# Attention in front of routed experts: q, k, v sets in up to four places on chip, loaded one transfer at a time, with five row buffers and another order of the first loads

## The chip, the cores and the metric

The kernel runs on one core of one Trainium2 chip. The metric is the device time of one execution in microseconds (us); lower is better. The kernel before took 1081.59 us (median of 3 runs, 1078.17 to 1083.07). TensorE is called PE here, VectorE DVE, ScalarE ACT, GpSimd POOL and SyncE SP; SP does no arithmetic, it issues transfers (DMAs).

## The reference

Three layers follow one another. The inputs are q, k and v of 4 batches, 8 heads, 576 positions and 64 columns.

```python
scores = scale * np.matmul(q, k.transpose(0, 1, 3, 2))
mask_plain = (rel >= 0) & (rel < 32)                                   # heads 0 to 3
mask_dil = (rel >= 0) & (rel < 128) & (rel % 4 == 0)                   # heads 4 to 7
attn = softmax(np.where(masks, scores, -1e9)); x = np.matmul(attn, v)  # then rows of 512 columns, 2304 of them
logits = x @ w_gate + np.log1p(np.exp(x @ w_noise)) * noise            # the best 2 of 8 experts for each row
out[mask] += top2_w[mask, k, None] * (np.maximum(x[mask] @ w1[e], 0.0) @ w2[e])
g = out @ w_gate2; y = (g * sigmoid(g) * (out @ w_val)) @ w_out
```

## The kernel before

**Stages.** The program is written out by hand in one order, and each engine executes its own instructions in that order. First comes attention with the routing of the first three quarters of the rows woven in (in the trace about 0 to 122 us), then the experts (to about 626 us), then the gated layer (to the end).

**Attention.** A *set* is the q, k and v of one batch b and one half t of the heads (t = 0 plain, t = 1 dilated): eight sets, each of 576 KB of q, 608 KB of k and 877.5 KB of v. A *unit* is two blocks of 64 queries: 36 units, nine for a batch. Units 9b to 9b+3 use set (b, 0), unit 9b+4 uses both, units 9b+5 to 9b+8 use set (b, 1). Unit u is therefore followed by the first use of (1, 0) at u = 9, of (1, 1) at 13, (2, 0) at 18, (2, 1) at 22, (3, 0) at 27 and (3, 1) at 31.

**One step.** `att_step(i)` (L691) is software-pipelined. On PE it issues the scores of unit i+1 (`at_S`: a mask matmul L183, then q times k L190), the product with v of unit i-1 (`at_AV`, L227), the turning of the normalised rows of unit i-2 (`at_XT`, L273) and the turning of the probabilities of unit i (`at_T`, L216). On DVE it issues the row maximum of unit i+1 (L198, L202), some small routing instructions (`go`), and then `at_norm` of unit i-1 (L256, L259, L262), whose last instruction writes the row tile `xs`. SP then stores `xs` to DRAM (`zd`, L267). `xs` has three buffers, so the rows of unit u wait until the store of unit u-3 has landed.

**Loads.** `load_qkv` (L87) issues q, k and v of one set on SP, back to back. The tiles of q, k and v have two buffers each in the pool `at`; so a set's transfers wait until the last reader of the set two before has finished, and SP, which issues in order, waits with them. The calls stand at L905 (before unit 5 of the batch) and L907 (before unit 1 of the batch). `load_raw` (L152) loads expert weights, `split` (L158) makes two parts of them on ACT and POOL. `late_consts` (L133) casts constants on DVE.

Of the kernel before, what the change touches and what calls it, by code (L numbers as in the profile page):

```python
# [20 lines left out]
N, DM, E, FF, F2 = 2304, 512, 8, 1024, 1536  # L21
NT = N // 128          # token tiles
NB = S // 64           # query blocks of one sequence
SEG = S // 4           # positions of one residue class
NA = N // 128          # most slot blocks of one expert
CAP = 640              # slots of one expert on the straight path
EARLY = 256            # first slots of experts 0 and 1, filled by batches 0 and 1 only
LOW = 384              # tokens of one block of the last layer
ID0 = 1024
# [11 lines left out]
def attn_moe_glu_kernel(ctx, tc, qT, kT, vB, cst, wgn, noise, wm, wz, out):  # L41
# [16 lines left out]

    # rows of x by token, then rows of y by slot (block, expert, row); a token with a slot past the
    # straight path finds its combined row in the place of its x  # L60
    zd = dr.tile([N + NA * E * 128, DM], F32, name="zd")
# [21 lines left out]

    # ------------------------------------------------------------ loads
    qt, kt, vt = {}, {}, {}

    def load_qkv(b, t, parts=1):  # L87
        q = qt[b, t] = at.tile([128, 2, S], F32, tag="q", bufs=2, name="q")
        k = kt[b, t] = at.tile([128, 2, 32 + S], F32, tag="k", bufs=2, name="k")
        v = vt[b, t] = at.tile([96, 4, NB, D + 1], F32, tag="v", bufs=2, name="v")  # L90
        cut = [0, S] if parts == 1 else [0, 128, S]
        for a, z in zip(cut, cut[1:]):
            SP.dma_start(q[:, :, a:z], qT[b, t, :, :, a:z])
            a2, z2 = (a + 32 if a else 0), z + 32
            SP.dma_start(k[:, :, a2:z2], kT[b, t, :, :, a2:z2])
            if z == cut[1]:
                SP.dma_start(v, vB[b, t])

    # dense work for the array while the first loads are on their way
    fill = gp.tile([128, 512], BF16, tag="g_ob", bufs=1, name="fill")  # L100
# [7 lines left out]
    busy(WARM[0])  # L108
    A.preload_act_table_set("natural_log_exp_and_others")
    ccon = gp.tile([128, C_MASK], F32, name="ccon")  # L110
    zs = gp.tile([128, N], F32, name="zs")
    SP.dma_start(ident, cst[:, 0:128])
    SP.dma_start(zs[:, 0:C_END - C_MASK], cst[:, C_MASK:])
    load_qkv(0, 0, parts=2)
    SP.dma_start(ccon[:, 128:C_MASK], cst[:, 128:C_MASK])
    wg = gp.tile([128, 4, 32], F32, name="wg")
    SP.dma_start(wg, wgn)
    nz = gp.tile([128, NT, E], F32, name="nz")
    SP.dma_start(nz, noise)
    load_qkv(0, 1)  # L120

# [22 lines left out]

    # ------------------------------------------------------------ expert weights
    segs = [(0, 0, EARLY), (1, 0, EARLY), (0, EARLY, CAP), (1, EARLY, CAP)] \
# [18 lines left out]

    # ------------------------------------------------------------ attention
    units = []
# [63 lines left out]
    def pieces(subs):  # L231
        """(partition, type, first token, step, count) of the rows of a unit"""
        res = []
        for sub, (t, j) in enumerate(subs):
            p = j * 64
            while p < j * 64 + 64:
                if t == 0:
                    n = j * 64 + 64 - p
                    tok, st = p, 1
                else:  # L240
                    n = min(j * 64 + 64, (p // SEG + 1) * SEG) - p
                    tok, st = 4 * (p % SEG) + p // SEG, 4
                q0 = sub * 64 + p - j * 64
                if res and res[-1][1] == t and res[-1][2] + res[-1][4] * st == tok:
                    res[-1][4] += n
                else:
                    res.append([q0, t, tok, st, n])
                p += n
        return res

    def at_norm(u):
        b, subs, _ = units[u]
        d = sav.pop(u)
        a3 = d[:, 0:260].rearrange("p (h k) -> p h k", h=4)
        den = at.tile([128, 4], F32, tag="den", bufs=2, name="den")
        V.tensor_scalar(den, a3[:, :, 64], 1e-9, None, op0=OP.add)  # L256
        go(1)
        rec = at.tile([128, 4], F32, tag="rec", bufs=2, name="rec")
        V.reciprocal(rec, den)  # L259
        go(1)  # L260
        x = sxs[u] = at.tile([128, 256], F32, tag="xs", bufs=3, name="xs")
        V.tensor_tensor(x.rearrange("p (h k) -> p h k", h=4), a3[:, :, 0:64],  # L262
                        rec[:, :, None].to_broadcast([128, 4, 64]), op=OP.mult)
        go(5)
        for q0, t, tok, st, n in pieces(subs):
            r0 = b * S + tok
            SP.dma_start(xd[r0:r0 + (n - 1) * st + 1:st, t * 256:t * 256 + 256], x[q0:q0 + n, :])  # L267
# [14 lines left out]

    # ------------------------------------------------------------ gating and routing
    groups = [(0, 4), (4, 9), (9, 13), (13, 18)]
# [7 lines left out]
    def regroup(o, src):  # L292
        """row 32 t + c of src to the rows 32 g + c of o's part t, for all g"""
        for t in range(4):
            T.matmul(o[:, t, :], lhsT=sel[:, t, :], rhs=src,
                     start=True, stop=True, skip_group_check=True)
# [244 lines left out]

    # the routing's small instructions, a few at a time between other work
    NEXT = "next"
# [22 lines left out]

    # ------------------------------------------------------------ expert layers
    xgt, xth, xtl, hps, hh_, hl_, yps = {}, {}, {}, {}, {}, {}, {}

    # column 4 p + k of a row belongs on partition p of chunk k: either PE turns a block of rows, or the  # L570
    # rows come in quarters, quarter g of the tokens 32 t + c on partition 32 g + c, and DVE turns 32 x 32
    def quarters(z):
# [8 lines left out]
    def turned(g, quarter, o=None):  # L581
        """a block of rows with its columns on partitions, [partition, chunk, row]"""
        if quarter:
# [10 lines left out]
    def parts(src, hi, lo, quarter, eng=V):  # L594
        """its two parts, on ACT and then on another engine"""
        how = "p k (t q) -> p k t q" if quarter else "p (k t) q -> p k t q"
# [92 lines left out]

    # ------------------------------------------------------------ emission: attention  # L690
    def att_step(i, turn):  # L691
# [3 lines left out]
        if i in FIRST_X:  # L695
            # the score bank has room for it
            tx = trans_x(0, FIRST_X.index(i), sT[i + 1][:, :, 192:448].rearrange("p a (c q) -> p a c q", c=2))
            next(tx)
# [32 lines left out]

    # the gated layer's weights, split once into two float32r parts
    cs = [{} for _ in range(3 * NK)]
# [14 lines left out]
    def cv_zero(n):  # L748
        if wide:
# [3 lines left out]
            A.activation(f, w1.bitcast(F32), AF.Abs)  # L753
            # 1 from the least normal number on, else 0
            A.activation(f, f, AF.Relu, scale=-2.0 ** 40, bias=least[0])
# [141 lines left out]

    LOADS = (10, 13, 16, 23, 25)
    SPLITS = (20, 22, 24, 26)
    for i in range(-1, NU + 2):  # L900
        u = i + 1
        b, r = divmod(u, 9)
        if 0 <= u < NU:
            if r == 5 and b + 1 < B:
                load_qkv(b + 1, 0)  # L905
            if r == 1 and b >= 1:
                load_qkv(b, 1)  # L907
        if 11 <= i < 38:
# [10 lines left out]
        if i < 1:  # L919
            busy(WARM[i + 2])  # L920
        if i == 1:
            late_consts()
# [10 lines left out]

    # ------------------------------------------------------------ emission: experts
    route.append([routing(3), True])
# [7 lines left out]

    # ------------------------------------------------------------ slots past the straight path
    rv = nc.values_load(most[0:1, 0:1], min_val=0, max_val=NA)
    with tc.If(rv > CAP // 128):  # L946
        with tc.tile_pool(name="ov", bufs=1) as ov:
            # rows that no expert computes
            none = ov.tile([128, E, DM], F32, name="none")
# [48 lines left out]

    # ------------------------------------------------------------ gated layer
    wp = ctx.enter_context(tc.tile_pool(name="wp", bufs=1))  # L1000
# [4 lines left out]
    def glu_gv(i):  # L1005
        b, f = st2[i]
        xh, xl = x2t[b]
        p = gvp[i] = bank2("AB"[i % 2])
        # what comes last from DVE or DRAM is used last
        parts = [(wh2[f], xh), (wh2[f], xl), (wl2[f], xh)] if i else [(wh2[f], xh), (wl2[f], xh), (wh2[f], xl)]  # L1010
# [19 lines left out]
    def glu_out(i):  # L1030
# [10 lines left out]
        if f == NK - 1:  # L1041
            for j in range(3):
                # the very last rows leave in two halves
                cut = (0, 256, 512) if b == NBLK - 1 and j == 2 else (0, 512)
# [111 lines left out]
```

## Time and profile before

| what | value |
|---|---|
| timed runs, median (lowest to highest) | 1081.59 us (1078.17 to 1083.07) |
| the profiled execution: span from its first to its last instruction | 1085.7 us |
| PE busy in the span | 1030.4 us (95%) |
| DVE, ACT, POOL busy | 667.9, 486.7, 441.3 us |
| HBM read and written | 121.37 MB and 38.80 MB |

The page gives no time for the profiled execution other than its span; it lies 4.1 us (0.4%) over the median of the timed runs. A busy PE is not a PE at full speed: "PEclk" in the tables is the share of the clock that was granted, so 1.00 means 2.4 GHz throughout and 0.66 means that a part of the stretch ran at 1.2 GHz.

### The profile page before, as it was taken

To read this page: it belongs to the slowest core of one execution; us is meant where nothing else is said; L and a number is where in the kernel's file an instruction comes from. 1 tells how busy PE (TensorE), PEld (TensorE's weight loads), DVE (VectorE), ACT (ScalarE), POOL (GpSimd) and SP (SyncE) were. 2 spreads that over 40 slices of the span, in tenths; PEclk is the share of its full clock that TensorE was granted. 3 is DMA by queue.
4 is the path that set the end of the run, shared out by engine and by line. 5 is a ranking of instruction groups with operands and counts; after the bars stand their busy time and mean duration, and the time that the engine had idled before them with its cause. 6 is when DMAs were issued, how large, how long until landed. Compare 5 with 4: busy or idle time off the path is not lost. (4 is left out here: it accounts for less than half of the span.)

```text
span 1085.7 us, 17127 instructions
## 1 busy us (share of the span) xinstructions
PE 1030.4 (95%) x6561; PEld 923.5 (85%) x6562; DVE 667.9 (62%) x1223; ACT 486.7 (45%) x909; POOL 441.3 (41%) x389
## 2 busy tenths in 40 slices
PE   7888989999998888988999999999999999999998
PEld 5676779999987877877789899999999999999997
DVE  3468777674999999998995634434335344244222
ACT  4666644454767766676664422223223222122111
POOL 0014156741688576785761247724315116000000
PEclk9888999999999998998999999999999999999999
DMA  7777346654577676775769668511101101100000
GB/s 234 222 225 231 109 141 217 190 180 157 186 237 240 201 263 190 248 250 185 247 202 327 185 221 293 193 49 27 54 11 37 42 10 43 36 1 1 30 1 29
DMA packets 59526, 161.34 MB, mean 149 GB/s; under 512 B 10032, under 2 KB 16560, under 8 KB 58672
## 3 DMA queue, kind: packets, MB, share of 16 engines
q1 hardware_dynamic: 46736, 121.27, 35.0%
q0 software_dynamic: 12560, 38.82, 11.0%
q8 instruction: 52, 0.85, 0.3%
q14 instruction: 34, 0.28, 0.1%
q10 hardware_dynamic: 144, 0.13, 0.0%
HBM read 121.37 MB, written 38.80 MB: 148 GB/s over the span
## 5 line engine op out<-in xcount | busy, mean ns | idle before, releaser
L579 POOL DMA_INDIRECT yg<-zd,row x126 | 124.6, 989 | 200.8 <-DVE yg L820 117.4
L579 POOL DMA_INDIRECT xg<-zd,idx x139 | 163.9, 1179 | 58.5 <-issue 32.5
L636 PE MATMUL bA<-xth,whi 128*128 128x320 f32 (+2 forms) x452 | 119.2, 322 | 32.6 <-DVE hlo L649 32.4
L164 DVE TENSOR_TENSOR wlo<-raw,whi 128x1024 fp32r<-128x1024 f32 x80 | 112.7, 1408 | 12.9 <-ACT whi L162 12.8
L636 PEld LDWEIGHTS bA<-xth,whi 128*128 128x128 f32 x452 | 80.9, 194 | 46.0 <-DVE hlo L649 43.0
L636 PE MATMUL bA<-xtl,whi 128*128 128x320 f32 (+2 forms) x452 | 115.9, 315 | 0.0
L636 PE MATMUL bA<-xth,wlo 128*128 128x320 f32 (+2 forms) x452 | 115.7, 314 | 0.0
L1023 DVE TENSOR_TENSOR t<-bB,ex 128x384 f32<-128x384 f32 x36 | 20.1, 557 | 134.4 <-ACT ex L1021 134.4
L162 ACT ACTIVATE whi<-raw 128x1024 fp32r<-128x1024 f32 x88 | 92.7, 1053 | 3.4 <-DMA raw<-in_wm 3.4
L757 POOL TENSOR_TENSOR cvw<-r,cvw 128x512 f32<-128x512 f32 x36 | 58.5, 1625 | 84.8 <-issue 46.9
L648 ACT ACTIVATE hhi<-bA 128x640 fp32r<-128x640 f32 (+2 forms) x73 | 42.2, 578 | 98.4 <-PE bA L636 98.1
L636 PEld LDWEIGHTS bA<-xtl,whi 128*128 128x128 f32 x452 | 81.0, 194 | 1.2 <-DVE xtl L601 0.2
L636 PEld LDWEIGHTS bA<-xth,wlo 128*128 128x128 f32 x452 | 80.5, 193 | 0.0
L649 DVE SCALAR_TENSOR_TENSOR hlo<-bA,hhi 128x640 fp32r<-128x640 f32 (+2 forms) x73 | 48.6, 666 | 51.9 <-ACT hhi L648 51.9
L1027 ACT ACTIVATE th<-t 128x384 fp32r<-128x384 f32 x72 | 37.8, 524 | 90.3 <-DVE t L1024 90.3
L1021 ACT ACTIVATE ex<-bB 128x384 f32<-128x384 f32 x36 | 17.7, 492 | 135.0 <-PE bB L1015 135.0
L1023 DVE TENSOR_TENSOR t<-bA,ex 128x384 f32<-128x384 f32 x36 | 19.9, 554 | 83.5 <-ACT ex L1021 83.5
L1028 DVE TENSOR_TENSOR tl<-t,th 128x384 fp32r<-128x384 f32 x72 | 40.3, 559 | 42.6 <-ACT th L1027 42.6
L599 ACT ACTIVATE xth<-xg 128x512 fp32r<-128x512 f32 x33 | 38.0, 1152 | 63.4 <-DVE xg L585 63.4
L1015 PE MATMUL bA<-x2h,wh 128*128 128x384 f32 x288 | 56.6, 338 | 0.5 <-PEq L946 0.3
L1021 ACT ACTIVATE ex<-bA 128x384 f32<-128x384 f32 x36 | 17.7, 492 | 87.6 <-PE bA L1015 86.5
L1015 PE MATMUL bB<-x2h,wh 128*128 128x384 f32 x288 | 56.4, 337 | 0.0
(232 smaller groups left out, 2639.2 us busy)
## 6 DMA issues: line engine op xcount, KB each, us to landing
raw<-in_wm SPq DMA_DIRECT2D x88, 512.0 KB, 4.2
r<-in_wz SPq DMA_DIRECT2D x36, 512.0 KB, 5.9
zd<-y SPq DMA_DIRECT2D x40, 256.0 KB, 5.4
whd<-cvhr SPq DMA_DIRECT2D x36, 256.0 KB, 4.7
wld<-cvlr SPq DMA_DIRECT2D x36, 256.0 KB, 4.7
wh<-whd POOLq DMA_DIRECT2D x12, 768.0 KB, 8.6
wl<-wld POOLq DMA_DIRECT2D x12, 768.0 KB, 8.8
v<-in_vB SPq DMA_DIRECT2D x8, 877.5 KB, 8.7
```

Source lines behind the costliest of these rows:

```text
L162: A.activation(whi[i], raw[i], AF.Copy)
L164: eng.tensor_tensor(wlo[i], raw[i], whi[i].bitcast(F32), op=OP.subtract)
L579: G.indirect_dma_start(out=g, out_offset=None, in_=src, in_offset=bass.IndirectOffsetOnAxis(ap=ix, axis=0))
L599: A.activation(hi, src, AF.Copy)
L636: T.matmul(hp[:, q, 0:cw], lhsT=wt[:, ws], rhs=xt[:, c, q * cw:q * cw + cw], start=c == 0 and j == 0, stop=c == 3 and j == 2)
L648: A.activation(a3, hp, AF.Relu)
L649: V.scalar_tensor_tensor(l3, hp, 0.0, a3.bitcast(F32), op0=OP.max, op1=OP.subtract)
L757: G.tensor_tensor(f, w1.bitcast(F32), f, op=OP.mult)
L1015: T.matmul(p[:, q, 0:LOW], lhsT=w[:, ws], rhs=x[:, c, :], start=c == 0 and j == 0, stop=c == 3 and j == 2, skip_group_check=True)
L1023: V.tensor_tensor(t, p[:, 0, 0:LOW], ex, op=OP.mult)
L1027: A.activation(a, t, AF.Copy)
L1028: V.tensor_tensor(l, t, a.bitcast(F32), op=OP.subtract)
```

## The change

- The sets (1, 0), (1, 1) and (3, 0) get their places in the pool `mp`, in the buffers that the experts' tiles `xth` and `xtl` use later. The others stay in the two buffers of the pool `at`.
- `load_qkv` becomes a generator that issues one transfer at a time. A table `SETS` says at which step of the attention loop a set's q is issued, and how many steps later k and v follow.
- The rows `xs` lie in the five buffers of the experts' tile `y`.
- The first loads: `ident` and `zs` are issued by ACT; SP begins with q and k of set (0, 0); its v comes after all of q and k, in two pieces (two blocks, then seven); set (0, 1) follows at once; `ccon`, `wg` and `nz` are issued in step 2 and cast in step 6.
- The first three loads of expert weights are issued in steps 15, 17 and 19 instead of 10, 13 and 16. Comments are gone, so line numbers move.

```diff
-    def load_qkv(b, t, parts=1):
-        q = qt[b, t] = at.tile([128, 2, S], F32, tag="q", bufs=2, name="q")
...
+    def load_qkv(b, t):
+        if (b, t) in ((1, 0), (1, 1), (3, 0)):
+            qk = mp.tile([128, 2, 32 + 2 * S], F32, tag="xth", bufs=2, name="qk")
+            q, k = qk[:, :, 0:S], qk[:, :, S:]
+            v = mp.tile([96, 4, NB, D + 1], F32, tag="xtl", bufs=2, name="v")
+        else:
+            q = at.tile([128, 2, S], F32, tag="q", bufs=2, name="q")
...
+        cut = [0, 128, S] if (b, t) == (0, 0) else [0, S]
         for a, z in zip(cut, cut[1:]):
             SP.dma_start(q[:, :, a:z], qT[b, t, :, :, a:z])
+            yield
             a2, z2 = (a + 32 if a else 0), z + 32
             SP.dma_start(k[:, :, a2:z2], kT[b, t, :, :, a2:z2])
-            if z == cut[1]:
-                SP.dma_start(v, vB[b, t])
+            yield
+        cut = [0, 2, NB] if (b, t) == (0, 0) else [0, NB]
+        for a, z in zip(cut, cut[1:]):
+            SP.dma_start(v[:, :, a:z, :], vB[b, t, :, :, a:z, :])
+            yield
...
-    SP.dma_start(ident, cst[:, 0:128])
-    SP.dma_start(zs[:, 0:C_END - C_MASK], cst[:, C_MASK:])
-    load_qkv(0, 0, parts=2)
-    SP.dma_start(ccon[:, 128:C_MASK], cst[:, 128:C_MASK])
...
+    A.dma_start(ident, cst[:, 0:128])
+    A.dma_start(zs[:, 0:C_END - C_MASK], cst[:, C_MASK:])
+    A.preload_act_table_set("natural_log_exp_and_others")
+    list(load_qkv(0, 0))
+    list(load_qkv(0, 1))
...
-        x = sxs[u] = at.tile([128, 256], F32, tag="xs", bufs=3, name="xs")
+        x = sxs[u] = mp.tile([128, 256], F32, tag="y", bufs=5, name="xs")
...
-    LOADS = (10, 13, 16, 23, 25)
+    SETS = {(1, 0): (0, 1), (1, 1): (3, 2), (2, 0): (8, 2), (2, 1): (13, 2), (3, 0): (18, 2), (3, 1): (24, 2)}
+    coming = {}
+    LOADS = (15, 17, 19, 23, 25)
...
-        if 0 <= u < NU:
-            if r == 5 and b + 1 < B:
-                load_qkv(b + 1, 0)
-            if r == 1 and b >= 1:
-                load_qkv(b, 1)
+        for bt, (i0, di) in SETS.items():
+            if i == i0:
+                coming[bt] = load_qkv(*bt)
+            if bt in coming and (i - i0) % di == 0:
+                next(coming[bt], None)
+        if i == 2:
+            SP.dma_start(ccon[:, 128:C_MASK], cst[:, 128:C_MASK])
+            SP.dma_start(wg, wgn)
+            SP.dma_start(nz, noise)
...
-        if i == 1:
+        if i == 6:
             late_consts()
```

What the program now asks of SP at its start. Here, and below, a row is one instruction: its line, its operation, out<-in, the shape, and in brackets the semaphores it waits for; DMAHW0 to DMAHW7 tell of landings, DVE and PE of those engines' work. First the kernel before:

```order
L112 DMA ident<-in_cst 128x128
L113 DMA zs<-in_cst 128x480
L93 DMA q<-in_qT 128x2x128
L95 DMA k<-in_kT 128x2x160
L97 DMA v<-in_vB 96x2340
L93 DMA q<-in_qT 128x2x448
L95 DMA k<-in_kT 128x2x448
L115 DMA ccon<-in_cst 128x444
L117 DMA wg<-in_wgn 128x128 [waits DMAHW0_49]
L119 DMA nz<-in_noise 128x144 [waits DMAHW1_49]
L93 DMA q<-in_qT 128x1152 [waits DMAHW2_49]
L95 DMA k<-in_kT 128x1216 [waits DMAHW3_49]
```

SP's start in the changed kernel, up to k of set (1, 0):

```order
L102 DMA q<-in_qT 128x2x128
L105 DMA k<-in_kT 128x2x160
L102 DMA q<-in_qT 128x2x448
L105 DMA k<-in_kT 128x2x448
L109 DMA v<-in_vB 96x4x130
L109 DMA v<-in_vB 96x4x455
L102 DMA q<-in_qT 128x1152 [waits DMAHW0_49]
L105 DMA k<-in_kT 128x1216 [waits DMAHW1_49]
L109 DMA v<-in_vB 96x2340 [waits DMAHW2_49]
L102 DMA qk<-in_qT 128x2x576 [waits DMAHW3_49]
L105 DMA qk<-in_kT 128x2x608 [waits DMAHW4_49]
```

The second pieces of q and k of set (0, 0) move ahead of its v, the constants are gone from here, and q and k of set (1, 0) stand before the first row store. In both kernels the eight landing semaphores go round, so a transfer also waits for the landing of the one eight places before it.

SP a little later, in the kernel before, from the first row store on:

```order
L267 DMA zd<-xs 128x256 [waits DMAHW5_49,DVE_49]
L267 DMA zd<-xs 128x256 [waits DMAHW6_49,DVE_49]
L267 DMA zd<-xs 128x256 [waits DMAHW7_49,DVE_49]
L93 DMA q<-in_qT 128x1152 [waits DMAHW0_49,PE_49]
L95 DMA k<-in_kT 128x1216 [waits DMAHW1_49]
L97 DMA v<-in_vB 96x2340 [waits DMAHW2_49,PE_49]
L267 DMA zd<-xs 128x256 [waits DMAHW3_49,DVE_49]
L267 DMA zd<-xs 64x256 [waits DMAHW4_49,DVE_49]
```

The same place in the changed kernel, from the first row store on:

```order
L278 DMA zd<-xs 128x256 [waits DMAHW5_49,DVE_49]
L109 DMA v<-in_vB 96x2340 [waits DMAHW6_49]
L923 DMA ccon<-in_cst 128x444 [waits DMAHW7_49]
L924 DMA wg<-in_wgn 128x128 [waits DMAHW0_49]
L925 DMA nz<-in_noise 128x144 [waits DMAHW1_49]
L278 DMA zd<-xs 128x256 [waits DMAHW2_49,DVE_49]
L102 DMA qk<-in_qT 128x2x576 [waits DMAHW3_49]
L278 DMA zd<-xs 128x256 [waits DMAHW4_49,DVE_49]
L278 DMA zd<-xs 128x256 [waits DMAHW5_49,DVE_49]
L105 DMA qk<-in_kT 128x2x608 [waits DMAHW6_49]
```

The transfers of sets (1, 0) and (1, 1) no longer wait for PE, they alternate with row stores, and the constants stand between the stores of units 0 and 1.

DVE around the casts of the constants, in the kernel before (after the rows of unit 0):

```order
L256 TENSOR_SCALAR den<-bd 128x4
L259 RECIPROCAL rec<-den 128x4
L262 TENSOR_TENSOR xs<-bd,rec 128x256
L134 CAST trib<-ccon 128x128
L135 CAST iotb<-ccon 128x128
L136 CAST iotc<-ccon 128x144
L137 COPY sel<-ident 128x512
L198 TENSOR_REDUCE nm<-bB 128x4
```

DVE around the same casts in the changed kernel (after the rows of unit 5):

```order
L267 TENSOR_SCALAR den<-be 128x4
L270 RECIPROCAL rec<-den 128x4
L273 TENSOR_TENSOR xs<-be,rec 128x256
L145 CAST trib<-ccon 128x128
L146 CAST iotb<-ccon 128x128
L147 CAST iotc<-ccon 128x144
L148 COPY sel<-ident 128x512
L209 TENSOR_REDUCE nm<-bA 128x4
```

The four instructions move five units later; behind them stands the row maximum of unit 8.

## Rows read from the trace of the kernel before

**Rows 1.** The page's first line.
```profile
span 1085.7 us, 17127 instructions
```

**Rows 2.** Busy time by stretch: start:end, length, engines, PEclk, DMA share, GB/s.
```profile
30.00:40.00 10.00, 7.64 (x88) 6.17 (x88) 3.58 (x14) 4.66 (x16) 0.00 (x0) 0.66 0.46 110
...
70.00:80.00 10.00, 10.00 (x170) 7.81 (x171) 7.24 (x36) 8.24 (x26) 2.35 (x1) 1.00 0.77 235
...
300.00:500.00 200.00, 174.62 (x925) 155.07 (x924) 195.45 (x228) 131.10 (x191) 145.23 (x109) 0.96 0.70 229
...
626.00:1086.00 460.00, 455.08 (x2378) 424.95 (x2376) 172.38 (x315) 114.18 (x232) 128.30 (x140) 1.00 0.19 64
```

**Rows 3.** Waits from 0 to 130 us: total us, times, longest.
```profile
DVE xs L262 <- DMA zd<-xs: 10.3, 4, 4.4
...
PE bB L190 <- DMA k<-in_kT: 6.1, 3, 3.9
```

**Rows 4.** Timeline of the start: start, length, instruction, count, [idle before <-releaser].
```profile
0.75 0.40 SPq L112 DMA_DIRECT2D ident<-in_cst  x1
...
6.54 0.56 PE L190 MATMUL bA<-k,q 64*64 64x96 f32 x16 [0.47 <-DMA k<-in_kT]
...
8.34 0.33 PE L183 MATMUL bB<-maskb,identb 128*128 128x192 bf16 x2
...
12.52 0.92 PE L190 MATMUL bB<-k,q 64*64 64x96 f32 x16 [3.85 <-DMA k<-in_kT]
...
15.95 0.56 PE L190 MATMUL bA<-k,q 64*64 64x96 f32 x16
```

**Rows 5.** DMA issues view, rate by half microsecond from 0 to 20 us.
```profile
GB/s 0 0 0 41 152 138 330 213 100 274 268 409 225 262 225 262 110 232 226 269 387 387 376 357 383 406 406 384 426 428 460 395 187 262 225 243 281 19 277 57
```

**Rows 6.** Timeline of two undisturbed steps (units 7 and 8).
```profile
26.49 0.56 PE L190 MATMUL bB<-k,q 64*64 64x96 f32 x16
...
27.12 0.56 DVE L198 TENSOR_REDUCE nm<-bB 128x4 f32<-128x384 f32 x1 [0.61 <-PE bB L190]
...
28.66 0.56 PE L190 MATMUL bA<-k,q 64*64 64x96 f32 x16
```

**Rows 7.** Timeline of units 9 to 13.
```profile
32.61 0.92 PE L190 MATMUL bB<-k,q 64*64 64x96 f32 x16 [1.71 <-DMA k<-in_kT]
...
34.77 0.42 DVE L262 TENSOR_TENSOR xs<-bd,rec 128x256 f32<-128x256 f32 x1 [4.37 <-DMA zd<-xs]
...
42.27 0.56 PE L190 MATMUL bA<-k,q 64*64 64x96 f32 x16
...
45.88 0.56 PE L190 MATMUL bB<-k,q 64*64 64x96 f32 x14 [0.53 <-DMA k<-in_kT]
```

**Rows 8.** Timeline near 62 us (rows of unit 15) and 77 us.
```profile
61.92 0.42 DVE L262 TENSOR_TENSOR xs<-be,rec 128x256 f32<-128x256 f32 x1 [3.72 <-DMA zd<-xs]
...
62.40 0.44 PE L273 MATMUL be<-ident,xs 128*128 128x128 f32 x2 [2.51 <-DVE xs L262]
...
77.10 0.42 DVE L262 TENSOR_TENSOR xs<-bd,rec 128x256 f32<-128x256 f32 x1 [1.17 <-DMA zd<-xs]
```

**Rows 9.** Timeline: first and last of the four casts.
```profile
18.07 0.22 DVE L134 CAST trib<-ccon 128x128 bf16<-128x128 f32 x1
...
18.48 0.42 DVE L137 COPY sel<-ident 128x512 f32<-128x512 f32 x1
```

**Rows 10.** Tile xs, 0 to 130 us: from issue of a row store to landing.
```profile
DMA to landing us min/median/max: 1.4/3.0/10.3
```

**Rows 11.** DMA issues, 0 to 130 us: count, KB each, median us to landing.
```profile
v<-in_vB SPq DMA_DIRECT2D x8, 877.5 KB, 8.7
k<-in_kT SPq DMA_DIRECT2D x7, 608.0 KB, 8.3
```

**Rows 12.** Timeline at 82 us: POOL and DVE.
```profile
82.18 2.35 POOL L164 TENSOR_TENSOR wlo<-raw,whi 128x1024 fp32r<-128x1024 f32 x1 [3.64 <-ACT whi L162]
82.20 2.38 DVE L352 SCALAR_TENSOR_TENSOR g_cc<-g_qq,ccon 128x40 f32<-128x40 f32 x1
```

More of the change, by code (lines that the diff above doesn't have):

```diff
@@ L85, in attn_moe_glu_kernel @@
     qt, kt, vt = {}, {}, {}
-    def load_qkv(b, t, parts=1):
-        q = qt[b, t] = at.tile([128, 2, S], F32, tag="q", bufs=2, name="q")
-        k = kt[b, t] = at.tile([128, 2, 32 + S], F32, tag="k", bufs=2, name="k")
-        v = vt[b, t] = at.tile([96, 4, NB, D + 1], F32, tag="v", bufs=2, name="v")
-        cut = [0, S] if parts == 1 else [0, 128, S]
+    def load_qkv(b, t):
[5 more added lines that the diff above has]
+            q = at.tile([128, 2, S], F32, tag="q", bufs=2, name="q")
+            k = at.tile([128, 2, 32 + S], F32, tag="k", bufs=2, name="k")
+            v = at.tile([96, 4, NB, D + 1], F32, tag="v", bufs=2, name="v")
+        qt[b, t], kt[b, t], vt[b, t] = q, k, v
+        cut = [0, 128, S] if (b, t) == (0, 0) else [0, S]
         for a, z in zip(cut, cut[1:]):
             SP.dma_start(q[:, :, a:z], qT[b, t, :, :, a:z])
+            yield
             a2, z2 = (a + 32 if a else 0), z + 32
             SP.dma_start(k[:, :, a2:z2], kT[b, t, :, :, a2:z2])
-            if z == cut[1]:
-                SP.dma_start(v, vB[b, t])
+            yield
[3 more added lines that the diff above has]
+            yield
     fill = gp.tile([128, 512], BF16, tag="g_ob", bufs=1, name="fill")
@@ L108, in attn_moe_glu_kernel @@
     busy(WARM[0])
-    A.preload_act_table_set("natural_log_exp_and_others")
     ccon = gp.tile([128, C_MASK], F32, name="ccon")
     zs = gp.tile([128, N], F32, name="zs")
-    SP.dma_start(ident, cst[:, 0:128])
-    SP.dma_start(zs[:, 0:C_END - C_MASK], cst[:, C_MASK:])
-    load_qkv(0, 0, parts=2)
-    SP.dma_start(ccon[:, 128:C_MASK], cst[:, 128:C_MASK])
     wg = gp.tile([128, 4, 32], F32, name="wg")
-    SP.dma_start(wg, wgn)
     nz = gp.tile([128, NT, E], F32, name="nz")
-    SP.dma_start(nz, noise)
-    load_qkv(0, 1)
+    A.dma_start(ident, cst[:, 0:128])
[3 more added lines that the diff above has]
+    list(load_qkv(0, 1))
     identb = gp.tile([128, 128], BF16, name="identb")
```

## Prediction

> **What bounds the kernel now.** I read the page first, then busy time by stretch, then the waits, then the timeline where the waits lie. The gated layer from 626 us on is PE's own time: PE is busy 455.08 of 460 us at the full clock [rows 2]. Nothing of the change touches it, nor the experts before it, which start when attention hands over. So the change is worth what attention gets shorter. An undisturbed step of attention takes 28.66 - 26.49 = 2.17 us from one unit's scores to the next [rows 6]. In 30 to 40 us PE has only 7.64 us of work and a granted clock of 0.66, DVE 3.58 us [rows 2]: the stage stands still. Two kinds of wait say why [rows 3]: DVE cannot write a row tile because a store has not landed (four times, 10.3 us), and PE waits for a set's k (three times in that bank, 6.1 us). The timeline shows how they hang together. The rows of unit 6 wait 4.37 us at 34.77 [rows 7], because the store of unit 3 stood in SP's queue behind the 877.5 KB of a v; a store needs 3.0 us in the median but up to 10.3 [rows 10], and three buffers cover only three steps, 6.5 us.
>
> **The change part by part.** The sum is made in the profiled execution (span 1085.7 us [rows 1], 0.4% above the median of the timed runs) and then taken off the median, 1081.59.
>
> *First loads.* Unit 1's scores start at 12.52, after 3.85 us of waiting for the second piece of k; PE itself was ready when its mask matmul ended, 8.34 + 0.33 = 8.67, or 2.13 after unit 0's scores at 6.54 [rows 4]. The running sum of the rate row puts v of set (0, 0) at about 5.0 to 8.5 us and the second pieces behind it [rows 5]. Without v in front they come 877.5 KB earlier: at v's 225 to 262 GB/s that is 3.4 to 4.0 us, so about 8.5 to 9.1. SP also no longer issues `ident` (0.40 us [rows 4]) and `zs` before q, up to 0.8 us more. I take unit 1's scores at 8.5: a gain of 4.0. Bounds: everything up to that piece (1488 KB) at only 225 GB/s from 2.0 us on, with half a microsecond to land, comes at 9.3, a gain of 3.2; with unit 0 also 0.8 earlier PE is ready at 7.8, a gain of 4.7. The cover of v: its first piece is wanted only a step and a half after unit 1's scores, and it is next in the queue.
>
> *Sets (1, 0) and (1, 1) without a wait for buffers, five row buffers.* From unit 8 to unit 12 the scores take 42.27 - 28.66 = 13.61 us [rows 6, 7]; four undisturbed steps are 8.68. The excess of 4.9 contains the wait for k (1.71), the row wait (4.37, partly beside it) and the slow PE after them (unit 9's scores take 0.92 instead of 0.56 us). All of it has the two causes that the change removes, so I take 4.9; the lower bound is the row wait alone, 4.4. Unit 13 waits another 0.53 for k [rows 7]: 0.5.
>
> *Five row buffers, later on.* At 61.92 DVE waits 3.72 us for a store, and PE 2.51 us behind it [rows 8]. DVE is full of routing instructions there, so the gain lies between these two and nearer to DVE's: 3.4. The other two row waits, 10.3 - 4.37 - 3.72 = 2.2 together, count nothing: the one at 77.10 [rows 8] lies in a stretch in which PE is busy 10.00 of 10.00 us [rows 2], and I treat the other alike.
>
> *Deadlines of the moved loads: nothing.* A set's pieces need 8.3 (k) to 8.7 us (v) from issue to landing in the median [rows 11]. The least lead in the new table is k of (3, 1), issued in step 26 and read in step 30: four steps, at least 8.7 us, in a stretch whose steps are longer because of routing. v of (3, 1) has four steps too, all others six to eight. The weights loaded in steps 15, 17 and 19 are split in steps 20, 22 and 24, five steps later. The places shared with the experts are read for the last time in units 17 and 31, before those tiles are written.
>
> *Constants later.* This is the term that costs. The casts take 18.48 + 0.42 - 18.07 = 0.8 us [rows 9] and move from the start, where PE was waiting anyway, into an undisturbed step, where DVE has 0.61 us of slack [rows 6]. And `ccon` now stands behind three whole sets: 304 + 3 x 2061.5 + 128 (a store) + 222 KB = 7.0 MB. At the mean of the rate row from 2.0 to 18.5 us, 294 GB/s [rows 5], it lands at 2.0 + 23.8 + 0.5 = 26.3. DVE comes to the casts 2.1 us after the scores of the unit two ahead (18.07 - 15.95 [rows 4, 9]), so about at 8.5 + 3.43 + 5 x 2.17 + 2.1 = 24.9 (3.43 is unit 1 to unit 2 [rows 4]). It waits 1.4, and unit 8's row maximum stands behind it, then unit 8's probabilities, then PE. Cost: 1.4 + 0.8 - 0.6 = 1.6. No such wait is in the trace; its bounds are 0 and the longest that DVE has for a landing, 4.4. This hides the next one: the store of unit 1, behind `ccon` and two small loads, must land before unit 6's rows, which come two steps after the casts' place.
>
> Sum: 4.0 + 4.9 + 0.5 + 3.4 - 1.6 = 11.2, hence 1081.6 - 11.2 = 1070.4. With all terms at their worst 3.2 + 4.4 + 0.5 + 2.5 - 4.4 = 6.2 (1075.4), at their best 4.7 + 4.9 + 0.5 + 3.7 = 13.8 (1067.8).
>
> **A rule against it.** v of set (0, 0) is now cut into runs of 520 and 1820 bytes. In the trace the runs of 1792 bytes (the second pieces of q and k, 10.0 to 12.5 us) move at 357 to 406 GB/s and v's whole runs of 9360 bytes at 225 to 262 [rows 5]: shorter runs were not slower. The Trainium skill (Perfetto Trace Analysis, section DMA Optimizations) says that transfers under 2 KB carry significant overhead each. By that rule the cut v would be slower than the uncut one, the constants later by what is lost, and the time would go towards the second rival's; by the row it is faster, and I follow the row.
>
> **Rivals.** *The unbroken stream starves DVE.* All loads run at the 225 GB/s that v shows. Then 7.0 MB take 31.1 us, `ccon` lands at 33.6, DVE reaches the casts at 9.3 + 3.43 + 10.85 + 2.1 = 25.7 and waits 7.9; the term of 1.6 becomes 8.1 and the first one 3.2: a gain of 3.9, 1077.7. For it speaks that v, 43% of a set, does run so slowly; against it, q and k from 10 us on.
>
> *DVE meets POOL at other places.* A routing instruction started beside POOL's part of a split takes 2.38 us, as long as POOL's own 2.35 [rows 12]; and from 300 to 500 us DVE is busy 195.45 of 200 us and PE idle 25.4 [rows 2]. If moved starts put more instructions into such meetings, a quarter more of that idle time costs 6.3: 1076.7. Against it: the splits stand at the same steps, and the experts' order is unchanged, so there is no reason for more rather than fewer. The Trainium skill (SBUF — State Buffer, section Who interferes with whom) says that a DVE instruction with two SBUF inputs waits out a POOL instruction that reads SBUF; the trace agrees with 2.38 us.
>
> *Slower: row stores starve behind single loads.* Stores and loads share SP's queue, and now a load stands between stores during nearly the whole stage. If each of the six later sets brought one row wait of the longest size, 4.37 us, DVE would wait 26.2 us instead of 10.3; less the start's 4.0 that is 11.9 slower, 1093.5. It decides once a store takes longer than five steps, 5 x 2.17 = 10.9 us, from row to landing; the longest now is 10.3 from its issue [rows 10], so the cover is thin for single stores, but the median is 3.0.
>
> **How the numbers follow.** The forecast gets 0.67, with its own range 1067.8 to 1075.4. The starving stream gets 0.14, POOL's meetings 0.10, starving stores 0.05; 0.04 is left for more than the best sum. A difference of about 0.5%, 5.4 us, is what a measurement of this kernel can tell from no change, so faster means under 1076.2. The forecast and the 0.04 lie there, with half of the second rival's and a seventh of the first's: 0.67 + 0.04 + 0.05 + 0.02 = 0.78. Within the bound are 0.12 + 0.05 = 0.17; slower 0.05. The range for eight in ten goes from 1065.5, the best sum less the spread of the timed runs, to 1079.5, which takes in the first two rivals.
>
> **What would show it.** In the changed kernel's profile: unit 1's scores at 8 to 9 us; units 9 to 13 at steps near 2.2 to 2.7 us, with no wait for k and the clock at 1.00 from 30 to 40 us; no row wait near 60 us; a wait of DVE for `ccon` of about 1 to 2 us near 25 us; the experts' first matmuls about 11 us earlier, and the gated layer the same 460 us long. It is wrong if DVE's row waits keep their 10 us, if the wait for `ccon` exceeds 5 us, or if attention ends 11 us earlier and the gated layer does not start so.

## The result: about 10.4 us faster, and where they came from

The changed kernel takes 1073.8 us (median of 20 runs; the lowest is 1068.48), the kernel before in the same comparisons 1083.23 us. The ratio is 0.9904, 95% interval 0.9884 to 0.9924, which is 10.4 us; the two medians lie 9.4 us apart. One of the 20 executions took 1990.31 us, which the ratio leaves out; its cause is not known. The forecast was 1070.4, a gain of 11.2, with a range of 1065.5 to 1079.5.

The page of the changed kernel, its first lines and the row of the granted clock (before: [rows 1], and PE busy 1030.4 us):

```profile
span 1072.6 us, 17127 instructions
...
PE 1022.9 (95%) x6562; PEld 919.1 (86%) x6562; DVE 664.6 (62%) x1223; ACT 486.2 (45%) x909; POOL 437.8 (41%) x389
...
PEclk9999999999999899999999999999999999999999
```

The profiled execution is 13.1 us shorter. Attention gives 11.3 of them: its last scores start at 106.13 instead of 117.41 us. The experts' stage gives 1.6, less than that stage differs from one kernel to another in which nothing of it was changed (below), and the gated layer is as long as it was. Busy time by stretch of the changed kernel, the last row being the gated layer (columns as in [rows 2]):

```profile
10.00:20.00 10.00, 9.28 (x163) 7.11 (x162) 5.50 (x22) 6.94 (x23) 0.00 (x0) 1.00 1.03 299
20.00:30.00 10.00, 8.03 (x157) 6.25 (x154) 4.91 (x20) 6.92 (x23) 0.00 (x0) 1.00 1.06 314
30.00:40.00 10.00, 9.55 (x144) 7.46 (x148) 6.07 (x21) 7.72 (x28) 0.00 (x0) 0.83 0.92 277
...
60.00:70.00 10.00, 9.97 (x178) 7.69 (x169) 7.77 (x38) 8.75 (x29) 2.35 (x1) 1.00 1.06 362
613.00:1073.00 460.00, 455.23 (x2379) 425.07 (x2377) 172.55 (x315) 114.07 (x232) 128.74 (x140) 1.00 0.19 64
```

From 30 to 40 us PE now has 9.55 us of work instead of 7.64, but not yet at the full clock (0.83). The gated layer's row is that of before to 0.15 us of PE [rows 2].

The waits on transfers between 0 and 130 us in the changed kernel (total, times, longest; before: [rows 3]):

```profile
DVE trib L145 <- DMA ccon<-in_cst: 3.4, 1, 3.4
...
PE bB L201 <- DMA k<-in_kT: 1.3, 1, 1.3
...
PE bA L201 <- DMA k<-in_kT: 0.7, 1, 0.7
```

The 10.3 us of row waits are gone; of the 6.6 us for k (6.1 in [rows 3], 0.5 at unit 0 [rows 4]) 2.0 are left; and one new wait is there: DVE waits 3.4 us for the constants. The start of each unit's scores, taken from the timelines, says where the kernel gets ahead of before:

| scores of unit | before, us | after, us | gained since the row above | forecast |
|---|---|---|---|---|
| 1 | 12.52 | 8.95 | 3.57 | 4.0 |
| 5 | 22.14 | 18.17 | 0.40 | 0 |
| 8 | 28.66 | 24.69 | 0 | 0 |
| 12 | 42.27 | 37.11 | 1.19 | 4.9 - 1.6 = 3.3 |
| 14 | 48.57 | 42.51 | 0.90 | 0.5 |
| 17 | 55.99 | 49.93 | 0 | 0 |
| 22 | 73.71 | 62.34 | 5.31 | 3.4 |
| 35, the last | 117.41 | 106.13 | -0.09 | 0 |

The total is 11.28, the forecast's 11.2; but two terms are wrong by 2 us each, in opposite directions. The timeline of the changed kernel around the first of them, DVE and then PE (columns as in [rows 4]):

```profile
24.29 0.42 DVE L273 TENSOR_TENSOR xs<-be,rec 128x256 f32<-128x256 f32 x1
28.07 0.23 DVE L145 CAST trib<-ccon 128x128 bf16<-128x128 f32 x1 [3.36 <-DMA ccon<-in_cst]
...
28.83 0.55 DVE L209 TENSOR_REDUCE nm<-bA 128x4 f32<-128x384 f32 x1
...
29.97 0.42 DVE L273 TENSOR_TENSOR xs<-bd,rec 128x256 f32<-128x256 f32 x1
```

```profile
27.47 0.69 PE L238 MATMUL be<-v,pT 96*64 96x65 f32 x16
30.45 0.44 PE L284 MATMUL bd<-ident,xs 128*128 128x128 f32 x2 [2.29 <-DVE xs L273]
...
31.41 0.83 PE L201 MATMUL bA<-qk 64*64 64x96 f32 x16
32.18 1.13 PE L238 MATMUL bd<-v,pT 96*64 96x65 f32 x16
...
35.03 0.56 PE L201 MATMUL bB<-qk 64*64 64x96 f32 x16
```

DVE is done with the rows of unit 5 at 24.71 and stands still until `ccon` lands; behind the casts stand the row maximum of unit 8 and the rows of unit 6, and PE stands 2.29 us until these rows can be turned. That is not all it costs: behind the pause the same matmuls take 1.13 instead of 0.69 us, the scores 0.83 instead of 0.56, at a granted clock of 0.83 in the stretch from 30 to 40 us: part of it at 1.2 GHz (0.50 from 32 to 34 us), the rest at 2.4. From unit 9 to unit 11 two steps take 35.03 - 26.86 = 8.17 us instead of 4.34.

### The profile page after: what moved, and what is told of

It reads as the page before. It is cut to its first block, busy times and chain, and to the rows that moved or that the text cites. A ratio compares the mean times of both kernels' runs of the same rounds, so it can differ in the third digit from the quotient of the medians.

```text
span 1072.6 us, 17127 instructions
## 1 busy us (share of the span) xinstructions
PE 1022.9 (95%) x6562; PEld 919.1 (86%) x6562; DVE 664.6 (62%) x1223; ACT 486.2 (45%) x909; POOL 437.8 (41%) x389
## 3 DMA queue, kind: packets, MB, share of 16 engines
q0 software_dynamic: 12560, 38.82, 10.9%
## 5 line engine op out<-in xcount | busy, mean ns | idle before, releaser
L175 DVE TENSOR_TENSOR wlo<-raw,whi 128x1024 fp32r<-128x1024 f32 x80 | 109.4, 1367 | 13.8 <-ACT whi L173 13.7
L768 POOL TENSOR_TENSOR cvw<-r,cvw 128x512 f32<-128x512 f32 x36 | 54.3, 1509 | 86.2 <-ACT cvw L767 60.2
L1033 PE MATMUL bB<-x2h,wl 128*128 128x384 f32 x288 | 56.4, 338 | 0.0
## 6 DMA issues: line engine op xcount, KB each, us to landing
v<-in_vB SPq DMA_DIRECT2D x7, 877.5 KB, 7.3
```

The source lines that it names most:

```text
L175: eng.tensor_tensor(wlo[i], raw[i], whi[i].bitcast(F32), op=OP.subtract)
L768: G.tensor_tensor(f, w1.bitcast(F32), f, op=OP.mult)
L1033: T.matmul(p[:, q, 0:LOW], lhsT=w[:, ws], rhs=x[:, c, :], start=c == 0 and j == 0, stop=c == 3 and j == 2, skip_group_check=True)
```

## The experiments

Each was timed in five rounds beside the kernel before on the same chip, and ratios are to that kernel; the experiments ran on three chips in all. The letters of the theories are explained in each expectation and hold for it alone. Times of single units, the start of the last scores too, come from one profiled execution each.

**Which part brings it.** Three kernels make one part of the change each, a fourth takes one back, and a fifth makes two of the three.

*Row buffers alone* (in the kernel before):

```diff
-        x = sxs[u] = at.tile([128, 256], F32, tag="xs", bufs=3, name="xs")
+        x = sxs[u] = mp.tile([128, 256], F32, tag="y", bufs=5, name="xs")
```

> The kernel before with one part of the change: the rows xs in five buffers. Theory A (the parts remove waits of their own): DVE's four row waits (10.3 us in the trace of before) go, of which 3.7 to 5.3 us near 62 us and about 3 near 35 us were paid; unit 9 still waits for k (1.7 us) and unit 1 starts at 12.5 as before. About 7 us faster than before, ratio 0.9935. Theory B (stores and loads share one queue, so more buffers only move the wait): row waits come back one or two units later; gain under 3 us, ratio over 0.997.

Measured: 0.9956 (0.9921 to 0.9992); last scores at 108.51, 8.9 us before those of the kernel before. There is no row wait; PE still waits for k four times, 6.7 us in all. From unit 8 to 12: 10.00 us (before 13.61), from 17 to 22: 12.40 (before 17.72). The waits went as the first theory has it; the ratio is a gain of 4.8 us, its interval 0.9 to 8.6.

*Places and table of the sets alone* (the changed kernel, with the first loads of before and three row buffers):

```diff
-        cut = [0, 2, NB] if (b, t) == (0, 0) else [0, NB]
-        for a, z in zip(cut, cut[1:]):
-            SP.dma_start(v[:, :, a:z, :], vB[b, t, :, :, a:z, :])
-            yield
+            if z == cut[1]:
+                SP.dma_start(v, vB[b, t])
+                yield
...
-    A.dma_start(ident, cst[:, 0:128])
+    SP.dma_start(ident, cst[:, 0:128])
...
     list(load_qkv(0, 0))
+    SP.dma_start(ccon[:, 128:C_MASK], cst[:, 128:C_MASK])
...
-        x = sxs[u] = mp.tile([128, 256], F32, tag="y", bufs=5, name="xs")
+        x = sxs[u] = at.tile([128, 256], F32, tag="xs", bufs=3, name="xs")
...
-        if i == 6:
+        if i == 1:
             late_consts()
```

> The kernel before with the sets part alone: up to four places, one transfer at a time by the table, first loads and casts in the order of before, three row buffers. Theory A: unit 9's wait for k goes, and a store stands behind one piece of a set, at most one v (about 3.6 us), instead of three pieces; but three buffers cover only 6.5 us, so some of the 10.3 us of row waits stays (half or more). About 4 us faster, ratio 0.996. Theory B: the queue is what matters, so singly spaced loads take nearly all row waits away without more buffers: about 9 us faster, ratio 0.992.

Measured: 0.9929 (0.9895 to 0.9964); last scores at 109.83, 7.6 us earlier. Behind unit 1 (3.6 us) there is no wait for k any more. Three row waits are left, 5.8 us in all, now at other places, two of them before unit 8's scores, here DVE of that kernel:

```profile
27.09 0.42 DVE L274 TENSOR_TENSOR xs<-be,rec 128x256 f32<-128x256 f32 x1 [2.96 <-DMA zd<-xs]
30.37 0.42 DVE L274 TENSOR_TENSOR xs<-bd,rec 128x256 f32<-128x256 f32 x1 [1.84 <-DMA zd<-xs]
```

From 17 to 22 it takes 12.39 us, as with the row buffers alone: here the two parts overlap, since a row store that stands behind a set is helped by more buffers and by spaced loads alike. At the last scores they gain 8.9 and 7.6 alone. The timed ratios (4.8 and 7.7 us) are too wide to show the overlap. Of the theories, the first was right on the waits (half or more stays), the second nearer on the gain.

*Order of the first loads and later constants alone* (in the kernel before):

```diff
-    SP.dma_start(ident, cst[:, 0:128])
+    A.dma_start(ident, cst[:, 0:128])
...
-            if z == cut[1]:
-                SP.dma_start(v, vB[b, t])
+        cut = [0, NB] if parts == 1 else [0, 2, NB]
+        for a, z in zip(cut, cut[1:]):
+            SP.dma_start(v[:, :, a:z, :], vB[b, t, :, :, a:z, :])
...
+        if i == 2:
+            SP.dma_start(ccon[:, 128:C_MASK], cst[:, 128:C_MASK])
...
-        if i == 1:
+        if i == 6:
             late_consts()
```

> The kernel before with the order of the first loads and the later constants alone (sets as before in two places, three row buffers). Theory A: unit 1's scores at about 9 instead of 12.5, set (0, 1) some 0.7 us late for unit 4; ccon stands behind two sets and lands near 21 us, before the casts at about 24, so DVE does not wait for it. The waits near 33 and 62 us stay. About 3.5 us faster, ratio 0.997. Rival: the start is given back at the next set's loads, which hang on buffers and on the queue: under 1 us, ratio 0.999 or more.

Measured: 0.9994 (0.9968 to 1.002), no gain shown. Unit 1 starts at 8.90 instead of 12.52, the last scores only 2.9 us earlier. With the old tables the time is waited for again, as in these two rows of PE:

```profile
41.26 0.56 PE L188 MATMUL bB<-k,q 64*64 64x96 f32 x14 [1.74 <-DMA k<-in_kT]
...
69.39 0.56 PE L188 MATMUL bA<-k,q 64*64 64x96 f32 x14 [2.67 <-DMA k<-in_kT]
```

*The changed kernel with three row buffers* (`tag="xs", bufs=3` in `at` again):

> The changed kernel with three row buffers instead of five. Theory A (five buffers carry the rows over the long landings behind the early stream): the store of unit 1 lands at 28.75 and unit 4 needs its buffer at about 22.2, so waits of 3 to 6 us come back before unit 9; later, where stores stand between single pieces, under 2 us in all. 3 to 6 us slower than the changed kernel, ratio about 0.994. Rival (spaced loads make the buffers superfluous): within 1 us of the changed kernel, ratio 0.990 to 0.991.

Measured: 0.9926 (0.9901 to 0.9951); five row waits, 7.2 us, and the last scores at 112.89. Here DVE:

```profile
25.96 0.42 DVE L273 TENSOR_TENSOR xs<-be,rec 128x256 f32<-128x256 f32 x1 [1.70 <-DMA zd<-xs]
31.17 0.42 DVE L273 TENSOR_TENSOR xs<-bd,rec 128x256 f32<-128x256 f32 x1 [3.77 <-DMA zd<-xs]
```

So the single loads don't let the stores through in time by themselves; the five buffers do it. In the timed ratio the difference to the changed kernel (0.9904) is 2.4 us, and the intervals overlap.

*Sets and row buffers without the new start* (the kernel of the second diff above, with five row buffers):

> The changed kernel with the first loads, the constants' loads and the casts in the order of before; sets and five row buffers as changed. Theory A (the earlier start is given back at the casts): unit 1's scores at 12 to 12.6, no wait for ccon, unit 12's scores at about 37 and attention's last scores at about 106 us, as in the changed kernel; ratio to before within 0.002 of the changed kernel's 0.990. Rival (the start's 4 us are kept): about 4 us slower than the changed kernel, last scores near 110, ratio about 0.994.

Measured: 0.9898 (0.9862 to 0.9934), level with the whole change. Its unit 1 starts as late as 13.96, behind a wait of 4.99 us for k, yet from unit 8 to 12 it needs 8.80 us, four undisturbed steps, and its last scores start at 107.19, only 1.06 after those of the changed kernel. The new start brings 5.0 us in this pair and keeps one, which is less than the changed kernel itself differs between two executions (2.8 us, below). Of a lead of 6.2 us at unit 8 the changed kernel loses 3.6 by unit 12, behind its wait for `ccon`, and another 1.5 from unit 26 to the last unit. That second loss is no wait for a load. The stretch from unit 29's scores to unit 32's in this kernel, in the changed one and in the one with the casts in step 10 (below; columns as in [rows 2]):

```profile
87.58:98.00 10.42, 8.42 (x144) 5.99 (x143) 9.54 (x45) 6.33 (x23) 3.69 (x3) 1.00 0.66 200
84.50:96.93 12.43, 9.91 (x144) 6.72 (x143) 10.92 (x45) 6.63 (x23) 4.20 (x3) 0.86 0.61 189
84.31:99.13 14.82, 12.41 (x143) 8.30 (x142) 10.92 (x45) 6.78 (x23) 4.21 (x3) 0.65 0.53 167
```

The same work takes PE 8.42, 9.91 or 12.41 us, at a granted clock of 1.00, 0.86 or 0.65, that is, with none, some or most of it at 1.2 GHz. Ahead of it PE waits several times for the routing's `g_oa`, at the longest 0.68 us in the first kernel and 1.16 in the other two. Why these waits fall differently in kernels whose routing is the same is not shown.

**What the constants cost.** Three kernels take DVE's wait for `ccon` away in three ways. None of their ratios differs from the changed kernel's by more than the intervals; what they show is in the traces.

*Casts in step 10:*

```diff
-        if i == 6:
+        if i == 10:
             late_consts()
```

> The changed kernel with the four casts in step 10 instead of 6. In the changed kernel DVE waits 3.36 us for ccon, which lands at 28.05; the stores of units 1 and 2 land at 28.75 and 30.57, and the rows of units 6 and 7 want their buffers at about 26.5 and 28.7. Theory A (the stream of the first three sets is late for whatever comes next): the wait moves to those rows, 2.2 us or a little less at unit 6; gain over the changed kernel at most 1.5 us, so ratio to before about 0.989. Rival (the casts alone cost it): 3.4 us faster than the changed kernel, ratio about 0.987, and no row wait in the trace.

Measured: 0.9893 (0.9858 to 0.9929). No wait for `ccon`, and in its place two short row waits (0.55 and 0.16 us) that PE does not feel; from unit 8 to 12 it takes 8.79 us instead of 12.42, by its waits nearer to the rival, by its ratio at theory A. But in its execution unit 4 waited 2.23 us for k instead of 0.66, and from unit 26 to the last it took 35.4 us instead of 33.0 (the slow stretch of the third row above), so that its last scores start at 108.33. The wait's price is shown, a gain in the end is not.

*`ccon` loaded between the first two sets:*

```diff
     list(load_qkv(0, 0))
+    SP.dma_start(ccon[:, 128:C_MASK], cst[:, 128:C_MASK])
     list(load_qkv(0, 1))
...
         if i == 2:
-            SP.dma_start(ccon[:, 128:C_MASK], cst[:, 128:C_MASK])
```

> The changed kernel, but ccon (222 KB) is issued between sets (0, 0) and (0, 1) instead of in step 2; its casts stay in step 6. Theory A (one instruction's wait: DVE's 3.36 us for ccon is what gave the start's gain back): no wait for ccon; unit 4 waits about 0.75 us more for k of (0, 1), since 222 KB at about 300 GB/s go ahead of it; units 5 to 12 take 16 to 17 us instead of 18.9, and the last scores start near 104.5 instead of 106.1; ratio to before 0.987 to 0.990. Theory B (the first 30 us are short of transfer rate, so a wait taken away here comes back at the next late piece): another wait of 1.5 us or more (k of (0, 1), the row store of unit 1, or v) stands in its place, unit 12 starts at 36.5 or later and the last scores near 106.

Measured: 0.9872 (0.9811 to 0.9933). On this chip the kernel before took 1103.82 us and the changed kernel, run beside it, 1089.54; this one took 1088.31. DVE and a stretch of it:

```profile
26.76 0.42 DVE L274 TENSOR_TENSOR xs<-be,rec 128x256 f32<-128x256 f32 x1
27.10 0.22 DVE L146 CAST trib<-ccon 128x128 bf16<-128x128 f32 x1
...
30.50 0.42 DVE L274 TENSOR_TENSOR xs<-bd,rec 128x256 f32<-128x256 f32 x1 [1.55 <-DMA zd<-xs]
```

```profile
30.00:40.00 10.00, 9.53 (x176) 7.14 (x176) 6.19 (x22) 8.36 (x31) 0.00 (x0) 1.00 0.87 278
```

The casts follow the rows at once, and the clock stays at 1.00. A row wait of 1.55 us stands in the place of 3.36, and from unit 8 to 12 it takes 9.20 us. From 5 to 12 that is 36.36 - 20.64 = 15.7 us, below the 16 to 17 of the first theory; the changed kernel beside it on this chip took 39.95 - 22.41 = 17.5. The second is right in part: something did come back at the next late piece, but half of it. The end did not come where the first theory put it: the last scores start at 106.32, not 104.5, since this execution began later (unit 1 at 10.10, unit 4 waiting 1.99 for k). Beside it the changed kernel began as late and had its last scores at 108.90.

*The next sets issued later:*

```diff
-    SETS = {(1, 0): (0, 1), (1, 1): (3, 2), (2, 0): (8, 2), ...
+    SETS = {(1, 0): (2, 2), (1, 1): (7, 2), (2, 0): (8, 2), ...
```

> The changed kernel with two entries of the table moved: set (1, 0) in steps 2, 4, 6 instead of 0, 1, 2, and (1, 1) in 7, 9, 11 instead of 3, 5, 7; casts in step 6 as changed. Theory A (what delays ccon and the first stores is the set in front of them): ccon lands near 22 us, DVE waits neither for it nor for a store, unit 12's scores at about 33.4 and the last at about 102.5; 3.5 us faster than the changed kernel, ratio about 0.987. Rival (the first two sets alone fill the queue): ccon lands after 25, wait of DVE over 1.5 us, ratio 0.989 to 0.990; or v of (1, 0), now in step 6, comes late for unit 9 and gives the same back.

Measured: 0.9900 (0.9863 to 0.9936). No wait for `ccon` and none for rows, 8.79 us from unit 8 to 12; but four waits for k and v (2.67 at unit 1, then 0.98, 0.46 and 0.59), and the last scores at 108.47. The wait for `ccon` went as theory A has it, the gain did not come.

**The last block of set (0, 1) first.** Unit 4 reads only the last 64 columns of q of (0, 1) and the last 96 of k, so these can be loaded ahead, on the table with later sets and on the changed kernel's own:

```diff
-        cut = [0, 128, S] if (b, t) == (0, 0) else [0, S]
-        for a, z in zip(cut, cut[1:]):
+        cut = {(0, 0): [(0, 128), (128, S)], (0, 1): [(S - 64, S), (0, S - 64)]}.get((b, t), [(0, S)])
+        for a, z in cut:
...
-            a2, z2 = (a + 32 if a else 0), z + 32
+            a2, z2 = (a, z + 32) if (b, t) == (0, 1) and a else (a + 32 if a else 0, z if (b, t) == (0, 1) else z + 32)
```

> As spaced, and of set (0, 1) the last block of q and k (64 and 96 columns, all that unit 4 reads) is loaded before the rest. Theory A: unit 4's wait for k (0.7 us in the changed kernel, 2.2 in the one with casts in step 10, 1.8 with the first loads alone) goes; 0.7 to 2 us faster than spaced, last scores near 101.5. Rival: two more transfers in the queue and the rest of k late for unit 5: no change to spaced.

Measured with later sets: 0.9866 (0.9824 to 0.9909), 1069.93 us, the last scores at 104.64 instead of the 101.5 expected: the fastest so far.

> The kernel with set (1, 0) spaced two steps apart, (1, 1) from step 7, and the last 64 columns of q and k of (0, 1) first, once more beside the changed kernel. If its 0.987 was no accident of one comparison: 0.985 to 0.988 again, 2 to 4 us below the changed kernel. If the noise of the experts' stage made it: 0.989 to 0.992, level with the changed kernel.

The same kernel on another chip: 0.9895 (0.982 to 0.9969), the second case of the two, though the interval takes in both. It is not shown to beat the changed kernel (0.9905 on the same chip).

> The changed kernel, but of set (0, 1) the last 64 columns of q and k are loaded first (unit 4 reads only these), the table SETS unchanged. Theory A: unit 4's wait for k (0.66 us, in other executions up to 2.23) goes, the two more transfers push ccon and the stores back a little, the wait for ccon stays at 3 us or more; unit 12 near 36.5 to 37. Theory B (supply of bytes): unit 4 as early, but what it gains is waited for at unit 5 or at ccon (4 us or more), unit 12 at 37 or later. Ratio to before about 0.990 by both.

With the table unchanged: 0.9869 (0.9807 to 0.9932), 1089.13 us beside 1089.54 for the changed kernel. Unit 4 doesn't wait, unit 5 starts at 17.80; then other waits follow, here PE's and DVE's:

```profile
21.64 0.68 PE L238 MATMUL bd<-v,pT 96*64 96x65 f32 x14 [0.84 <-DMA v<-in_vB]
```

```profile
27.02 0.42 DVE L273 TENSOR_TENSOR xs<-be,rec 128x256 f32<-128x256 f32 x1 [2.06 <-DMA zd<-xs]
...
30.34 0.23 DVE L145 CAST trib<-ccon 128x128 bf16<-128x128 f32 x1 [2.89 <-DMA ccon<-in_cst]
```

Unit 12 starts at 39.48, 2.4 us later than in the changed kernel's first profile and 0.5 before its second, on the same chip (below). What unit 4 gains is waited for later, as the second theory had it.

> The changed kernel once more, beside the others on one chip. Expected 0.990 of before (0.988 to 0.993); unit 1's scores between 8.5 and 10.5, unit 4's wait for k between 0.5 and 2.3, a wait for ccon of 1 to 3.5 us: how much the start varies from one execution to another.

Measured: 0.9905 (0.9866 to 0.9944), as at first. In its execution unit 1 starts at 10.40, unit 4 waits 2.3 us for k, DVE 2.97 for `ccon`, and the last scores start at 108.90. So the start of one and the same kernel moves by 1.5 us from one execution to another, and attention's end by 2.8; the kernel before took 1083.23 us in the comparisons of the first and 1103.82 beside the second, so what the chip adds is not shown. From the last scores to the gated layer it took 503 to 510 us in the other executions and 510 to 514 in the three of this chip described here, though nothing in it was changed; the gated layer took 459 us and, on this chip, 466. That is why differences of 2 us in attention don't show in the ratios.

## Why the forecast held, step by step

*What bounds it.* Right: the gated layer kept its time, attention ended 11.3 us earlier and the rest came forward by as much and 1.6 more. The step of 2.17 us [rows 6] is the undisturbed one after too.

*First loads, 4.0.* Measured 3.57 at unit 1 (8.95, behind a wait of 1.28 for k) and 3.97 by unit 5. The later bound for unit 1, 9.3, was too good: other executions had it at 10.10 and 10.40. The step from unit 1 to unit 2, taken over as 3.43, was 2.09, which is 1.34 gained; unit 4's wait for k (0.66), which I had not priced, made the next step 3.11 instead of 2.17 and took 0.94 of that back. The term stood right through errors that cancel, which is luck. Nor is it a gain in the end: the kernel without the new start is level with the whole change.

*Sets and buffers, 4.9, and unit 13, 0.5.* The 4.9 is right: in three kernels that have both and no wait for `ccon` there (casts in step 10, sets and row buffers without the new start, sets issued later), units 8 to 12 take 8.79 or 8.80 instead of 13.61, a gain of 4.8. Unit 13 gave 0.90 instead of 0.5: the step with its wait of 0.53 had been longer by that much. That I gave the row buffers their own term is not borne out: the stretch from 17 to 22 becomes as short with either part alone. Only the two together were predicted, and together they remove these waits.

*Constants, -1.6.* This step failed in its size: from unit 8 to 12 the changed kernel takes 12.42 us, 3.6 more than without the wait. DVE came when I said (24.71; forecast 24.9). The landing was 1.8 late, 28.07 instead of 26.3, and not because the transfers were slow. The DMA view of the changed kernel from 0 to 28.05 us:

```profile
DMA packets 4052, 7.55 MB, mean 269 GB/s; under 512 B 302, under 2 KB 2984, under 8 KB 3858
```

From 2.0 us on that is 7.55 MB in 26.05 us, 290 GB/s where I had taken 294. What was wrong is that I counted only the 7.0 MB ahead of it: another half a megabyte had moved, and what SP had issued behind `ccon` by then was `wg`, `nz`, a row store and q of (1, 1). At 290 GB/s 0.55 MB are 1.9 us. Here the landing has to be reckoned with everything that is under way at the same time, not only with what was issued before. With the measured wait the forecast's own sum gives 3.36 + 0.8 - 0.6 = 3.56, so the late landing is nearly the whole error of 2.0 us. The way there was still another: of DVE's 3.36 us only 2.29 reached PE as a pause, and the rest of the excess over four undisturbed steps, 3.74 - 2.29 = 1.45, is the slower PE behind it, for which the forecast had no term. That these two nearly cancel is luck.

*The row wait near 62 us, 3.4.* This term was too small: it left out the slower PE behind a pause. Of the 5.31 us measured, 7.48 - 4.81 = 2.67 are from unit 17 to 19, which answers to PE's pause of 2.51 [rows 8]; the other 10.24 - 7.60 = 2.64 are from unit 19 to 22, in which the kernel before ran behind this pause with a clock of 0.66 from 60 to 70 us (0.50 from 64 to 70). The row buffers alone win both back: 12.40 us from unit 17 to 22. PE of the kernel before, from the next unit on:

```profile
63.47 0.92 PE L190 MATMUL bB<-k,q 64*64 64x96 f32 x16
64.32 1.13 PE L227 MATMUL be<-v,pT 96*64 96x65 f32 x16
```

The bound from both sides, 2.5 to 3.7, looked at waits only and could not hold it. In the changed kernel the stretch 60 to 70 us runs at 1.00. The two errors, a cost 2.0 us too small and a gain 1.9 too small, have different sources, a landing reckoned too early and a slow stretch left out. That they cancel, so that the total comes to 11.3 beside 11.2, is luck.

*The rule against it.* The Trainium skill (Perfetto Trace Analysis, section DMA Optimizations) speaks of overhead below 2 KB. The changed kernel's rate by half microsecond from 0 to 20 us:

```profile
GB/s 0 0 0 57 142 142 369 349 233 65 129 351 362 361 349 332 276 267 240 226 237 217 279 271 332 408 424 428 416 424 239 206 262 262 243 140 231 263 336 362
```

By the bytes ahead of it, v of set (0, 0), in runs of 520 and 1820 bytes, moved from about 7.7 to 11.3 us, at 217 to 279 GB/s; the uncut v had 225 to 262 [rows 5]. The trace shows no loss, and `ccon` was late by bytes, not by rate. No run has the new order with v uncut.

*The rivals.* The starving stream: its rate (225 GB/s throughout) did not come, and its wait of 7.9 us came out at 3.4. POOL's meetings: attention from unit 22 on is as long as before, and the experts' stage was 1.6 shorter in this pair. Starving stores: a row store's way has a median of 4.2 us instead of 3.0, the longest is 8.3, under the 10.9 from which it decides. With three buffers this rival is real (five row waits); with five, other executions show single ones of 0.16 to 2.06.

*Of the marks named,* unit 1 at 8 to 9, the row wait near 60, the experts' 11 us (11.3 at the last scores) and the gated layer came as said. The wait for `ccon` is 3.36 instead of 1 to 2, and units 9 to 13 don't have their steps nor the clock of 1.00 that I named, because of it.

## What to carry to other kernels

A wait that starves PE can cost more than its pause, namely the slow instructions behind it: look at the granted clock of the stretch behind the pause and count both, for a wait that goes and for one that comes. A transfer issued late may land by all the bytes under way until then, later ones included. Give a small constant that an in-order engine will wait for a place ahead of the big sets, not behind three of them: on the same chip that took units 5 to 12 from 17.5 to 15.7 us, though no gain in the whole time is shown. Parts that relieve the same queue need not add up: at the last scores of one execution each, 8.9 and 7.6 alone made 10.2 together (the kernel with both), and a start made 5 us faster kept 1 us.

## What the runs showed of the hardware

The loads take longer when more of them are under way, though the rate is no lower. The DMA issues of the changed kernel from 0 to 30 us (count, KB each, median us from issue to landing; before: [rows 11]):

```profile
v<-in_vB SPq DMA_DIRECT2D x2, 877.5 KB, 14.0
...
ccon<-in_cst SPq DMA_DIRECT2D x1, 222.0 KB, 13.9
...
nz<-in_noise SPq DMA_DIRECT2D x1, 72.0 KB, 12.5
```

A v of 877.5 KB took 14.0 us instead of 8.7, and the 72 KB of `nz` took hardly less. From 20 to 30 us the transfers carried 314 GB/s; the kernel before had 294 from 2.0 to 18.5 us [rows 5]. What an early load costs is then the landing time of everything small beside it, row stores included: from 18 to 40 us the median of theirs was 6.4 us, of the whole stage 4.2. A store can also stand in SP before its issue: the rows of unit 1 were written at 15.08 us, but their store was issued only at 20.41, since SP first waited, 4.0 us of them, for the landing of v of set (0, 1), issued eight transfers ahead at 6.25; it landed at 28.75.
